# A wait between two stages of swapped halves: VectorE copies replaced by an empty TensorE instruction

## The chip, the cores and the metric

The kernel runs on one core of a Trainium2 chip. The metric is the device time of one execution in microseconds, as the median of several runs. Before the change it is 2585.78 us (three runs, 2584.07 to 2587.34). All times below are in us unless ns is written.

## The reference

The block takes x (2048 rows of 576), a fused weight for queries, keys and values, an output weight, and three weights of a gated feed-forward layer of width 4608.

```python
xn = _layernorm(x, axis=-1)
s = _A_ref(xn, A_wqkv, A_wo)               # 32 heads of 18, softmax over 2048 keys, then @ wo
g = _silu(_B_ref(xn, B_w_gate, B_w_up, B_w_down))   # (gelu(xn @ w_gate) * (xn @ w_up)) @ w_down
return x + s * g
```

Everything is float32 in and out.

## The kernel before

**Numbers.** Each float32 operand of the large products is split into a high and a low float16 part, and a product is the sum of three float16 products: high by high, high by low, low by high. For a contraction of 576 rows that makes 12 products over four full blocks of 128 rows and one or two more for the last 64 rows.

**Halves.** TensorE's rows are used as two halves of 64. A product whose operands lie on partitions 0 to 63 runs in the upper half at the same time as one on partitions 64 to 127 in the lower half. The kernel keeps the two from writing the same PSUM bank at once: two results are built together, in two banks. In stage 0 the upper half adds its 64 contraction rows to result one and the lower half adds its rows to result two; in stage 1 the halves are swapped, the upper one adding to result two and the lower one to result one. Three classes work so: `Pair` (L462; queries and keys, gate and up; tiles ma and mb, 14 slots in stage 0 and 13 in stage 1, products at L492), `DownPair` (L730; the down projection, one two-bank tile md, 6 slots of 288 columns in each stage, products at L752), and `OutPair` (L878; the output projection, either md or ma and mb, 14 slots or 17, products at L931). There are 160 such pairs, 288 down pairs and 16 output pairs in the program.

**The swap.** Stage 1's first product writes a bank that stage 0's last product, in the other half, has just written. Before stage 1 the kernel therefore waits until that last product is in. It does so with `touch` (L456 to L460): VectorE copies one element, or one from each of the two banks, out of PSUM into a small tile. The copy waits for the last product that wrote the bank, and the first product of stage 1, which writes the bank that the copy reads, waits for the copy. An output pair in two tiles, whose two halves end at different slots, copies from the bank or the banks that matter.

**Order.** The order of all instructions is written out by hand; each engine works its own queue in that order. The main loop goes over pairs of heads. At each step TensorE computes a score block for the exponentials (`qk2`, L1395, read by ScalarE's exponential at L1401), then one for the row maxima of a later pair of heads (`qk1`, L1343, read by VectorE's reduction at L1346), then part of the feed-forward work: perhaps one stage of a down pair (`DownPair.run`), then some slots of the pair in hand (`g_run`). Every five steps or so a burst (L1420) multiplies the collected exponentials with the values. A pair's stage 1 does not begin before another score block has been issued since its stage 0 ended (`blocks[0] <= gs.end`), so some other work of TensorE lies between the two stages of nearly every pair.

**The planner.** How many slots and which stages of down pairs go into each step of a stretch is chosen by `make_plan`. It tries all layouts of 4 to 7 steps and takes the one with the least sum, most of which comes from `lost`, a model of when TensorE and VectorE would be free. In it a down stage that does not end its pair, and the end of a pair's stage 0, keep VectorE until the products are done plus TOUCH:

```python
if d:
    vec = max(vec, e1 + D_STAGE) + (EVAC if late else TOUCH)
...
elif first:
    vec = max(vec, t) + TOUCH
```

**The end.** After the feed-forward layer come the output pairs, between the last score blocks and bursts of the last pair of heads; the gate (L795, L799), the evacuation of an output pair (L968, L975) and the normalisation of the last heads (L1443 to L1452) run on ScalarE and VectorE in between.

Of the kernel before, what the change touches and what calls it, by code (L numbers as in the profile page):

```python
# [12 lines left out]
F32 = mybir.dt.float32  # L13
# [81 lines left out]
def kernel(ctx: ExitStack, tc: tile.TileContext, x, wqkv, wo, w_gate, w_up, w_down, out):  # L95
    nc = tc.nc
# [4 lines left out]
    sm = ctx.enter_context(tc.tile_pool(name="sm", bufs=3))  # L101
    wp = ctx.enter_context(tc.tile_pool(name="wp", bufs=2))
    ap = ctx.enter_context(tc.tile_pool(name="ap", bufs=2))
# [349 lines left out]

    banks = deque([("ma", "mb")])

    def touch(ap):  # L456

        t = sm.tile([1, 2], F32, tag="touch", name="touch", bufs=2)
        o = t[:, 0:1] if len(ap.shape) == 2 else t.rearrange("p (a b) -> p a b", a=2)
        nc.vector.tensor_copy(o, ap)  # L460

    class Pair:  # L462

# [23 lines left out]

        def slot(self):

            for o, terms in self.q:  # L490
                lw, xx = terms[self.k]
                nc.tensor.matmul(  # L492
                    o, lw, xx, start=self.stage == 0 and self.k == 0,
                    stop=self.stage == 1 and self.k == self.slots - 1, skip_group_check=True,
                )
            self.k += 1
            if self.k < self.slots:
                return False
            if self.stage == 0:
                touch(self.b.t[0:1, 0:1])  # L500
            self.stage += 1
            if self.stage == 2:
                self.end(self.a, self.b)
            return True
# [225 lines left out]
    class DownPair:  # L730
# [8 lines left out]
        def run(self):  # L739

            w, c, sb, si = self.args
            hs = hstate[c, sb]
            sl = slice(P * si, P * si + P)
            if self.stage == 0:
                self.t = MTile("md", [P, 2, 512], F32, 1)
            k = 0
            for ft in range(2):
                for a, b in ((hs.hi, w.dhi), (hs.hi, w.dlo), (hs.lo, w.dhi)):
                    for half in range(2):
                        r = slice(64 * half, 64 * half + 64)  # L750
                        hf = half ^ self.stage
                        nc.tensor.matmul(  # L752
                            self.t.t[:, hf, 0:288], a[r, ft, sl], b[r, ft, 288 * hf:288 * hf + 288],
                            start=self.stage == 0 and k == 0, stop=self.stage == 1 and k == 5,
                            skip_group_check=True,
                        )
                    k += 1
            if self.stage == 0:
                touch(self.t.t[0:1, :, 0:1])
            self.stage += 1  # L760
            return self.stage == 2

# [115 lines left out]
    class OutPair:  # L878
# [47 lines left out]
        def slot(self):  # L926

            for half, (o, terms) in enumerate(self.q):
                if self.k < len(terms):
                    a, b = terms[self.k]  # L930
                    nc.tensor.matmul(  # L931
                        o, a, b, start=self.stage == 0 and self.k == 0,
                        stop=self.stage == 1 and self.k == len(terms) - 1, skip_group_check=True,
                    )
                    last = half
            self.k += 1
            if self.k < self.slots:
                return False
            if self.stage == 0:
                if self.wide:  # L940
                    touch(self.t[0].t[0:1, :, 0:1])
                else:
                    for o in self.o[1:] if last else self.o[::-1]:
                        touch(o[0:1, 0:1])
            self.stage += 1
            if self.stage == 2:
                self.evac()
            return True
# [283 lines left out]
    with tc.manual_schedule():  # L1232
# [23 lines left out]
        for t in range(2):  # L1256
            ln_scale(t)
            ln_hi(t)
            ln_lo(t)
        stats(7)  # L1260
        run(pw[:5])
        ln_tr(0)
        ln_out(0)
        run(pw[5:6])
        stats(4)
        run(pw[6:8])
        for t in range(2, 4):
            ln_scale(t)
# [258 lines left out]
    k = 0  # L1527
# [35 lines left out]
    dn = None  # L1563
    gs.closed = False
    G_SLOT, D_STAGE, BLOCK, BURST = 0.2158, 0.735, 0.43, 2.9
    ROW_MAX, EVAC, ADD, TOUCH = 1.28, 0.86, 0.75, 0.15
    LEAD = 0
    KEEP_HALF, KEEP_END = 2, 4
    whole = (NPAIR - 1) * 4 * NT
# [115 lines left out]
    for p in range(NPAIR):  # L1685
# [3 lines left out]
        for i in range(4 * NT):  # L1689
            s, half = divmod(i, 2)  # L1690
# [175 lines left out]
```

## Time and profile before

| | |
|---|---|
| median of three runs | 2585.78 |
| lowest, highest | 2584.07, 2587.34 |
| span of the profiled execution, first to last instruction | 2583.5 |
| mean granted TensorE clock in it | 0.997 |
| TensorE busy | 2503.6 (97%), 25816 matmuls |
| VectorE busy | 1894.5 (73%), 2595 instructions |
| of this in L460's copies | 65.4, 466 instructions |
| ScalarE, GpSimd busy | 1660.4 (64%), 1536.8 (59%) |

The profile is of one execution; the page gives its span, and the runs give whole times, whose median lies 2.3 over that span. A matmul's end in the trace is modelled, and matmuls overlap, so TensorE counts as busy through short stops; the distance from one matmul's start to the next shows them. "PE" is TensorE's matmuls, "PEld" its weight loads, "DVE" VectorE, "ACT" ScalarE, "POOL" GpSimd; a name with q is the engine's sequencer. In a timeline row stand start, duration, engine, line, operation, written tile and read tiles, shape and count, and in brackets how long the engine sat idle before it and what ended that. In the view of a tile stand durations in ns (least, median, most) with first and last start, then what the engine idled for before these instructions (us, times), then who waited for them.

### The profile page before, as it was taken

The page shows a single profiled execution, that of the slowest core. Times are in us where ns is not written, and L with a number is a line of the kernel's source. Part 1 is how long each engine was busy: PE and PEld are TensorE (multiplying, and loading weights), DVE is VectorE, ACT ScalarE, POOL GpSimd, SP SyncE. Part 2 cuts the span into 40 slices and gives each one's busy share as a digit, 9 for nine tenths or more (in the row PEclk, how much of TensorE's full clock was granted, in tenths as well). Part 3 has the DMA queues.
Part 4 walks back from the last instruction along what each step waited for, and adds up shares of the span by engine and source line. Part 5 has one row for each costly group of instructions (what it writes and reads, how often), then busy time and mean ns, then how long its engine had stood idle before and what let it go on. Part 6 is the DMA issues. An engine that isn't in the chain of part 4 may idle for free.

```text
span 2583.5 us, 60864 instructions
## 1 busy us (share of the span) xinstructions
PE 2503.6 (97%) x25816; PEld 1316.9 (51%) x25816; DVE 1894.5 (73%) x2595; ACT 1660.4 (64%) x2082; POOL 1536.8 (59%) x1545
## 2 busy tenths in 40 slices
PE   7899999999999999999999999999999999999998
PEld 6554445444544454445445545454544555455555
DVE  7677768777787778777777777776777777777644
ACT  6126666766677666766666666667666666766664
POOL 4346664576357564667576675848576676757513
PEclk9999999999999999999999999999999999999999
DMA  4430121201130112111110111201111111010124
GB/s 154 132 94 21 19 55 43 75 14 29 52 87 16 22 45 63 32 38 47 19 52 16 33 40 29 56 11 37 29 34 29 38 22 45 9 49 12 37 63 139
DMA packets 134635, 118.69 MB, mean 46 GB/s; under 512 B 59691, under 2 KB 113713, under 8 KB 134362
## 3 DMA queue, kind: packets, MB, share of 16 engines
q1 hardware_dynamic: 130089, 106.39, 15.8%
q0 software_dynamic: 1568, 5.37, 0.6%
q8 instruction: 202, 3.31, 0.5%
q10 hardware_dynamic: 2704, 3.03, 0.4%
q14 instruction: 72, 0.58, 0.1%
HBM read 84.89 MB, written 29.61 MB: 44 GB/s over the span
## 4 chain that ended last, share of the span: by engine, by line
PE 82%; DVE 7%; POOL 3%; ACT 3%; issue 2%; DMA 2%; SPq 0%; ACTq 0%; POOLq 0%; DVEq 0%
PE mb_t L492 16%; PE md_t L752 15%; PE ma_t L492 15%; PE md_t L1420 9%; PE s L1395 8%; PE s L1343 8%; PE ma_t L1420 6%; DVE PM L1346 3%; ACT P L1401 1%; PE md_t L931 1%; DVE osb L1428 1%; DMA QT<-QD 1%; POOL raw_c L356 1%; PE pv_t L511 1%; PE mb_t L931 1%
## 5 line engine op out<-in xcount | busy, mean ns | idle before, releaser
L1346 DVE TENSOR_REDUCE PM<-s 128x2 f32<-128x1024 f32 x1024 | 1251.0, 1224 | 335.5 <-PE s L1343 327.6
L1401 ACT ACTIVATE P<-s,etab 128x1024 f32<-128x1024 f32 x896 | 995.6, 1112 | 590.2 <-PE s L1395 579.4
L492 PE MATMUL ma_t<-XHT,whi_c 64*128 64x512 f16 x1440 | 542.0, 376 | 4.3 <-DVE osb L1428 2.2
L492 PE MATMUL mb_t<-XHT,whi_c 64*128 64x512 f16 x1440 | 541.7, 376 | 2.3 <-DVE touch L460 1.5
L492 PE MATMUL ma_t<-XHT,wlo_c 64*128 64x512 f16 x1296 | 487.4, 376 | 0.0
L492 PE MATMUL ma_t<-XL,whi_c 64*128 64x512 f16 x1152 | 433.2, 376 | 0.0
L492 PE MATMUL mb_t<-XHT,wlo_c 64*128 64x512 f16 x1152 | 433.2, 376 | 0.0
L492 PE MATMUL mb_t<-XL,whi_c 64*128 64x512 f16 x1152 | 433.0, 376 | 0.0
L1395 PE MATMUL s<-QT,KT 56*128 56x512 f16 x2048 | 404.4, 380 | 6.6 <-ACT P L1401 2.6
L1343 PE MATMUL s<-KT,QT 54*128 54x512 f16 x2048 | 398.3, 378 | 12.0 <-DVE PM L1346 9.7
L492 PEld LDWEIGHTS <-whi_c 64*128 64x128 f16 x5184 | 273.9, 94 | 241.0 <-issue 19.3
L752 PE MATMUL md_t<-dhi_c,hhi 64*128 64x288 f16 x2304 | 341.3, 283 | 4.8 <-DVE touch L460 2.1
L752 PE MATMUL md_t<-dhi_c,hlo 64*128 64x288 f16 x2304 | 341.0, 282 | 0.0
L752 PE MATMUL md_t<-dlo_c,hhi 64*128 64x288 f16 x2304 | 340.5, 282 | 0.0
L752 PEld LDWEIGHTS <-hhi 64*128 64x128 f16 x4608 | 246.7, 94 | 140.4 <-issue 16.8
L715 POOL TENSOR_TENSOR hlo<-gv,hhi 128x512 f16<-128x512 f32 x144 | 167.3, 1162 | 215.0 <-ACT hhi L708 210.7
L693 POOL TENSOR_SCALAR tw<-tw 128x512 f32<-128x512 f32 x144 | 90.7, 630 | 341.2 <-ACT tw L686 340.9
L1420 PE MATMUL md_t<-P,VT 128*32 128x512 f32 x2472 | 291.9, 596 | 0.5 <-ACT P L1401 0.5
L1395 PEld LDWEIGHTS <-KT 56*128 56x128 f16 x2048 | 123.5, 94 | 244.2 <-issue 156.4
L680 POOL TENSOR_TENSOR tw<-gs 128x512 f32<-128x512 f32 x144 | 151.0, 1049 | 125.2 <-ACT gs L657 125.1
L772 DVE SCALAR_TENSOR_TENSOR y<-md_t,c_c,y 128x576 f32<-128x576 f32 x272 | 219.5, 807 | 8.2 <-PE md_t L752 8.2
L492 PEld LDWEIGHTS <-wlo_c 64*128 64x128 f16 x2592 | 138.0, 94 | 118.9
(270 smaller groups left out, 4061.5 us busy)
## 6 DMA issues: line engine op xcount, KB each, us to landing
draw_c<-in_B_w_down SPq DMA_DIRECT2D x18, 576.0 KB
raw_c<-in_B_w_gate SPq DMA_DIRECT2D x18, 512.0 KB
raw_c<-in_B_w_up SPq DMA_DIRECT2D x18, 512.0 KB
obr<-rd SPq DMA_DIRECT2D x30, 256.0 KB
KT<-KD SPq DMA_DIRECT2D x32, 224.0 KB
QT<-QD SPq DMA_DIRECT2D x32, 216.0 KB
VS<-vst POOLq DMA_DIRECT2D x16, 304.0 KB, 2.6
VT<-VS SPq DMA_DIRECT2D x16, 304.0 KB
```

Source lines behind the costliest of these rows:

```text
L492: nc.tensor.matmul(o, lw, xx, start=self.stage == 0 and self.k == 0, stop=self.stage == 1 and self.k == self.slots - 1, skip_group_check=True,
L680: gp.tensor_tensor(st["t"], st["g"], st["g"], op=ALU.mult)
L693: gp.tensor_scalar(st["t"], st["t"], 1.0, 1.0, op0=ALU.mult, op1=ALU.add)
L715: gp.tensor_tensor(hs.lo[:, ft], st["v"], hs.hi[:, ft], op=ALU.subtract)
L752: nc.tensor.matmul(self.t.t[:, hf, 0:288], a[r, ft, sl], b[r, ft, 288 * hf:288 * hf + 288], start=self.stage == 0 and k == 0, stop=self.st ...
L772: nc.vector.scalar_tensor_tensor(yy, y, w.c, yy, op0=ALU.mult, op1=ALU.add)
L931: nc.tensor.matmul(o, a, b, start=self.stage == 0 and self.k == 0, stop=self.stage == 1 and self.k == len(terms) - 1, skip_group_check=True,)
L1343: nc.tensor.matmul(s1[:, h], QT[p][r, P * qt:P * qt + P], KT[p][r, 512 * kb:512 * kb + 512], start=True, stop=True)
L1346: nc.vector.tensor_reduce(PM[p][:, :, qt, kb:kb + 1], s1, op=ALU.max, axis=AX.X)
L1395: nc.tensor.matmul(s2[:, h], KT[p][r, P * kt:P * kt + P], QT[p][r, 512 * qb:512 * qb + 512], start=True, stop=True)
L1401: nc.scalar.activation(pt, s2, AF.Exp, scale=ETAB[j0])
L1420: nc.tensor.matmul(t.t[qd:qd + 32, :], VT[p][:, c0:c0 + 32], pt[:, h], start=kt == k0, stop=kt == k1, skip_group_check=True,)
```

## The change

The copies go. In their place `follow` puts an empty instruction on TensorE's own queue just ahead of stage 1's first product, and makes it wait for the last product of stage 0, which each class now remembers in `self.last`. `nofuse` keeps the instruction from being folded into a neighbour. In an output pair `last` is the last product issued in either half. The planner's TOUCH becomes zero. The rest of the program text is the same.

```diff
-    def touch(ap):
-
-        t = sm.tile([1, 2], F32, tag="touch", name="touch", bufs=2)
-        o = t[:, 0:1] if len(ap.shape) == 2 else t.rearrange("p (a b) -> p a b", a=2)
-        nc.vector.tensor_copy(o, ap)
+    def follow(earlier):
+
+        tc.add_manual_dep(
+            nc.tensor.nop(hint="swap", nofuse=True).ins, earlier.ins.name,
+            mybir.DependencyInfo(mybir.DependencyClass.Sync, mybir.DependencyReason.DATA),
+            reason="the halves change banks",
+        )
...
         def slot(self):
 
-            for o, terms in self.q:
+            for half, (o, terms) in enumerate(self.q):
                 lw, xx = terms[self.k]
-                nc.tensor.matmul(
+                if self.stage and half == self.k == 0:
+                    follow(self.last)
+                m = nc.tensor.matmul(
                     o, lw, xx, start=self.stage == 0 and self.k == 0,
                     stop=self.stage == 1 and self.k == self.slots - 1, skip_group_check=True,
                 )
...
             if self.stage == 0:
-                touch(self.b.t[0:1, 0:1])
+                self.last = m
...
-                        nc.tensor.matmul(
+                        if self.stage and half == k == 0:
+                            follow(self.last)
+                        m = nc.tensor.matmul(
                             self.t.t[:, hf, 0:288], a[r, ft, sl], b[r, ft, 288 * hf:288 * hf + 288],
...
             if self.stage == 0:
-                touch(self.t.t[0:1, :, 0:1])
+                self.last = m
...
-                    nc.tensor.matmul(
+                    if self.stage and half == self.k == 0:
+                        follow(self.last)
+                    m = nc.tensor.matmul(
                         o, a, b, start=self.stage == 0 and self.k == 0,
                         stop=self.stage == 1 and self.k == len(terms) - 1, skip_group_check=True,
                     )
-                    last = half
+                    last = m
...
             if self.stage == 0:
-                if self.wide:
-                    touch(self.t[0].t[0:1, :, 0:1])
-                else:
-                    for o in self.o[1:] if last else self.o[::-1]:
-                        touch(o[0:1, 0:1])
+                self.last = last
...
-    ROW_MAX, EVAC, ADD, TOUCH = 1.28, 0.86, 0.75, 0.15
+    ROW_MAX, EVAC, ADD, TOUCH = 1.28, 0.86, 0.75, 0.0
```

## The prediction

> **What bounds the kernel now.** I read the page first, then busy time by stage, then the view of the tile the copies write, and last the timeline around single swaps.
>
> ```profile
> span 2583.5 us, 60864 instructions
> PE 2503.6 (97%) x25816; PEld 1316.9 (51%) x25816; DVE 1894.5 (73%) x2595; ACT 1660.4 (64%) x2082; POOL 1536.8 (59%) x1545
> 250.00:600.00 350.00, 345.32 (x3510) 1.00 0.16 39
> 600.00:1000.00 400.00, 392.29 (x4011) 1.00 0.17 42
> 1000.00:1500.00 500.00, 492.06 (x5021) 1.00 0.15 40
> 1500.00:2000.00 500.00, 495.04 (x5168) 1.00 0.13 31
> 2000.00:2400.00 400.00, 396.35 (x4138) 1.00 0.11 28
> ```
>
> The five windows give, in this order, their bounds, length, TensorE's busy time (matmuls), granted clock, DMA share and GB/s. From 250 to 2400 us it is idle 4.7 + 7.7 + 7.9 + 5.0 + 3.7 = 29 us of 2150. So TensorE sets the end, and whatever VectorE does is worth only what TensorE is made to wait for it. VectorE's 73% busy is no gain in itself.
>
> The copies:
>
> ```profile
> L460 DVEq EVENT_SEMAPHORE  x337: 21/21/21, 214.1 to 2547.4; - x169
> L460 DVE COPY touch<-md_t x294: 135/138/149, 224.3 to 2569.3; 1x2 f32<-1x2 f32 x147
> L460 DVE COPY touch<-mb_t x169: 134/146/148, 151.8 to 2574.9; 1x1 f32<-1x1 f32 x169
> ...
>   PE mb_t L492: 21.0, 58
>   PE md_t L752: 19.0, 43
> ...
>   POOL E_c L326: 7.2, 3
>   PE md_t L931: 2.7, 2
>   PE mb_t L492: 2.3, 7
>   PE mb_t L931: 2.2, 3
>   PE md_t L752: 2.1, 2
>   PE pv_t L492: 0.6, 1
> ```
>
> With three more copies (two of ma_t, one of pv_t) there are 466, of about 0.14 us: 65 us of VectorE, plus 337 semaphore instructions of 21 ns (7 us) and 47 us in which VectorE stands idle at the head of its queue until TensorE's last product is in (40 us of it in the two rows quoted). The last five PE rows are what TensorE visibly pays: 9.9 us. There are 464 swaps: 160 projection and gate/up pairs, 288 down pairs, 16 output pairs (two of these copy twice).
>
> **Where a copy costs TensorE, and where not.** A swap that is covered:
>
> ```profile
> 1007.32 0.29 PE L752 MATMUL md_t<-dhi_c,hlo 64*128 64x288 f16 x2
> 1007.65 0.15 DVE L460 COPY touch<-md_t 1x2 f32<-1x2 f32 x1 [0.29 <-PE md_t L752]
> 1007.66 0.38 PE L1343 MATMUL s<-KT,QT 54*128 54x512 f16 x2
> 1007.67 0.32 PEld L752 LDWEIGHTS <-hhi 64*128 64x128 f16 x4
> 1007.88 0.29 PE L752 MATMUL md_t<-dhi_c,hhi 64*128 64x288 f16 x2
> ```
>
> The last product of stage 0 starts at 1007.32 and ends at 1007.61; two score blocks run meanwhile; the copy is through at 1007.80, and stage 1 starts at 1007.88, the usual 0.22 us after the score block. Nothing is lost. A swap that is not:
>
> ```profile
> 1495.90 0.29 PE L752 MATMUL md_t<-dhi_c,hlo 64*128 64x288 f16 x2
> ...
> 1496.24 0.38 PE L1343 MATMUL s<-KT,QT 54*128 54x512 f16 x2
> 1496.30 1.22 DVE L319 TENSOR_SCALAR E_c<-mg_c 128x2 int32<-128x2 int32 x1
> ...
> 1497.51 0.14 DVE L460 COPY touch<-md_t 1x2 f32<-1x2 f32 x1
> 1497.57 1.20 DVE L1346 TENSOR_REDUCE PM<-s 128x2 f32<-128x1024 f32 x1
> 1497.70 0.30 PE L752 MATMUL md_t<-dhi_c,hhi 64*128 64x288 f16 x2 [1.07 <-DVE touch L460]
> ...
> 1499.94 0.40 PE L1343 MATMUL s<-KT,QT 54*128 54x512 f16 x2
> ```
>
> The product was in at 1496.19, but the copy stood behind 1.22 us of other VectorE work; TensorE began 0.05 us after the copy's end, 1497.70 - 1496.24 - 0.22 = 1.24 us late. The idle column shows 1.07 of this, because the modelled end of the previous matmul covers about 0.16. So I count from start to start, less the usual spacing after that block (0.22 after a score block, 0.12 after a 288-column pair), over all swaps whose stage 1 begins within 60 ns of their copy's end. There are 50; the first and the last:
>
> ```profile
> 151.77 0.14 DVE L460 COPY touch<-mb_t 1x1 f32<-1x1 f32 x1 [0.31 <-PE mb_t L492]
> 151.97 0.37 PE L492 MATMUL mb_t<-XHT,whi_j 64*126 64x512 f16 x1
> 2574.92 0.14 DVE L460 COPY touch<-mb_t 1x1 f32<-1x1 f32 x1 [0.30 <-PE mb_t L931]
> 2575.12 0.28 PE L931 MATMUL mb_t<-whi_wo,ohl 64*128 64x288 f16 x1 [0.23 <-DVE touch L460]
> ```
>
> Their excess is 7.2 us in 25 pair swaps, 3.8 in 16 down swaps and 6.1 in 9 output swaps: **17.1 us**. That is the whole direct price of the copies.
>
> **What is added: 464 empty instructions on TensorE's queue.** Each waits until the last product of stage 0 is in, and nothing behind it is issued before: the weight loads and products of stage 1, then the next score block, for which ScalarE (exponentials) and VectorE (row maxima) wait. No DMA hangs on that queue's place. What counts is L, the time from the modelled end of the last product to the start of the first of stage 1. The trace has no such instruction; the nearest row is a semaphore wait on the same queue:
>
> ```profile
> L1420 PEldq EVENT_SEMAPHORE  x17: 51/51/51, 218.9 to 2552.7; - x17
> ```
>
> It takes 51 ns (VectorE's takes 21). Around it I put what the copies show: about 40 ns from a product's end to the copy's start (1007.61 to 1007.65), and 53 ns from its end to the matmul. So L lies between 0.12 (40 + 21 + 53, rounded up) and, with the queue's own 51 ns and as much again to fetch the first weight load behind it, 0.19 us (40 + 51 + 51 + 53). I take **0.19**, since nothing behind the wait is prefetched. What hides it is the work between the stages. For all but 15 swaps that cover is at least 0.235 us after the last product's end (in the covered case 1007.88 - 1007.61 = 0.27; some 110 swaps lie so; some 340 have 0.4 us or more, most of them 0.9, with other products between; the 15 have one score block or none). At L = 0.12 the 15 short swaps pay 1.5 us together, at 0.19 2.6 us. If the cover is outrun it costs: at 0.30, 7 us over 119 swaps; at 0.38, 17; at 0.50, 33.
>
> [...]
>
> **What is handed back.** Where TensorE no longer waits, the next thing it needs of VectorE is the row maximum of the score block it ran, behind which the copy stood. In the stall above that reduction ends at 1498.77 and the next score block starts at 1499.94, so 1.1 us earlier is possible. Over the 41 pair and down stalls the slack is at least the excess in all but a few: I take off 1.0 us.
>
> **The output stage** has the longest stop:
>
> ```profile
> 2504.43 0.40 PE L1395 MATMUL s<-QT,KT 56*128 56x512 f16 x2
> 2507.33 0.30 PE L931 MATMUL md_t<-whi_wo,ohl 64*128 64x288 f16 x2 [2.50 <-DVE touch L460]
> 2507.57 0.42 PE L931 MATMUL md_t<-whi_wo,ohl 64*128 64x288 f16 x4
> 2509.12 0.72 PE L931 MATMUL md_t<-whi_wo,ohl 64*128 64x288 f16 x4
> 2508.00:2511.30 3.30, 3.30 (x29) 2.44 (x27) 0.36 (x1) 2.08 (x3) 0.00 (x0) 0.50 0.02 5
> ```
>
> The stop is 2507.33 - 2504.43 - 0.22 = 2.68 us, and then the granted clock is 0.50 for 3.3 us (0.42 us becomes 0.72), which loses half of that, 1.7 us. Without the stop both go. But the chain of gate, evacuation and next burst behind it still runs on ScalarE and VectorE; I take off 1.3 us for that in this stage.
>
> [...]
>
> **The planner's constant.** TOUCH goes from 0.15 to 0 in the sums by which each stretch of 4 to 7 steps is laid out. The order of some stretches will change, by differences of at most 0.15 per down start or gate/up swap in a sum that stays otherwise the same. What it can move is the idle time that remains: from 250 to 2400 us 29 us, of which the copies' stalls in those windows are about 8.5. I value it at nothing and keep 7 us (a third of the rest) either way for the range.
>
> **The freed VectorE time** (119 us) meets TensorE's other waits for VectorE only where a copy stands just ahead of the late result; I take 0, with 4 us at most.
>
> **The sum**: 17.1 + 1.7 (clock) - 2.6 (rest of the wait) - 1.0 - 1.3 = 13.9 us less. The span becomes 2583.5 - 13.9 = 2569.6. The timed runs before have a median of 2585.78, 2.3 us over the span of the profiled execution (start and end around it), which stays: 2571.9, **2572 us**, 0.5% faster.
>
> **Rivals.**
> 1. *The stall is handed on.* VectorE is late with the same work, so TensorE next waits for the row maximum instead. Then each of the 41 stalls gains only the copy's 0.14 us: 5.7, less 2.6 for the wait, 3.1: 2583. For it: the reductions follow the copies without a gap (1497.57). Against: the slack of 1.1 us at 1499.94.
> 2. *The wait is dearer than its cover*, which is the slower side: the queue behind the empty instruction restarts slowly, and about 120 swaps with only the score blocks between their stages pay L - 0.27 each. The gross gain without the term for the rest of the wait is 16.5; it is used up at L = 0.38. At 0.50 the swaps pay 33: 2585.8 + 16.2 = 2602. Against it stand the 51 ns row and, at 218.9, that semaphore waits on this queue run ahead of the products. Were the queue emptied at each swap, score blocks included, every swap would stop for some 0.38 us and the time would be about 2750; I give that 2 of 100 within this case.
> 3. *The new order is worse.* The re-planned stretches add as much idle time as the steady part has beside the copies, 29 - 8.5 = 20 us: 2572 + 20 = 2592; half of it: 2582.
> 4. *The gain is larger*: the order and the freed VectorE each give their bound, 2572 - 7 - 4 = 2561.
> 5. *No wait is put on the instruction* (the dependency lies within one engine). Then the rest of the wait goes too, 2569, inside the forecast.
>
> **Chances.** Forecast, 2565 to 2579: 55. Rival 4: 10. Rival 1: 17 (12 within 0.2%, 5 below). Rival 2: 8. Rival 3: 10 (5 within, 5 slower). A measurement of this kernel tells about 0.2%, 5.2 us, from no change. So faster 0.55 + 0.10 + 0.05 = 0.70; same 0.12 + 0.05 = 0.17; slower 0.08 + 0.05 = 0.13. For 8 in 10 the range goes from rival 4's bound, 2560, to past rival 1 and half of rival 3: 2588.
>
> **What would show it.** No copies at L460; VectorE busy near 1829 us; 464 more entries on TensorE's queue, some 50 ns each. At the late swaps the first product of stage 1 follows the score block by 0.22 us. No half clock near 2508. PE's idle time from 250 to 2400 falls from 29 to about 21 us. I am wrong if the first products of covered swaps come 0.3 us or more after the score block (L too small), if waits for L1346 rise by as much as the copies' go (handed on), or if idle time rises at other places (order).

## The result, and the profile after

The changed kernel takes 2568.68 us (median of five runs, 2568.55 to 2572.9) against 2585.78: the ratio is 0.9941, with a 95% interval of 0.993 to 0.9951. That is about 17 us, or 0.6%. The forecast was 2572 us, 14 us less than before. Of all executions of the kernels below one, of order_alone, was far slower than its fellows (2779.96 us, at a mean granted clock of 0.893, the others at 0.997), and it is left out of its ratio.

The page of the changed kernel, its first two lines of numbers:

```profile
span 2566.9 us, 60550 instructions
PE 2495.3 (97%) x25816; PEld 1301.0 (51%) x25816; DVE 1854.4 (72%) x2129; ACT 1662.3 (65%) x2082; POOL 1540.4 (60%) x1545
```

The 466 copies are gone from VectorE (2595 instructions became 2129). Its busy time fell by only 40 us, although the copies measured 65: a copy overlapped the instruction behind it (in the prediction's rows, 1497.51 + 0.14 = 1497.65, and the reduction begins at 1497.57), and the page counts such a stretch once.

Busy time by stage, in the five steady windows (bounds, length, TensorE's busy time and matmuls, the same for weight loads, VectorE, ScalarE and GpSimd, then granted clock, DMA share and GB/s):

```profile
250.00:600.00 350.00, 344.56 (x3508) 171.79 (x3502) 259.62 (x291) 233.00 (x270) 209.53 (x211) 1.00 0.17 39
600.00:1000.00 400.00, 393.41 (x4027) 200.07 (x4025) 299.23 (x338) 276.34 (x378) 234.42 (x243) 1.00 0.17 43
1000.00:1500.00 500.00, 493.46 (x5065) 243.42 (x5063) 375.57 (x412) 334.81 (x389) 323.52 (x319) 1.00 0.15 39
1500.00:2000.00 500.00, 494.96 (x5156) 248.08 (x5154) 368.35 (x397) 343.00 (x452) 339.13 (x333) 1.00 0.14 31
2000.00:2400.00 400.00, 397.11 (x4132) 206.32 (x4128) 292.33 (x313) 268.07 (x312) 265.54 (x260) 1.00 0.11 29
```

TensorE is idle 5.4 + 6.6 + 6.5 + 5.0 + 2.9 = 26.5 us in them; before it was 29. The fall is small because much of a stall was never counted as idle, as the prediction said of the modelled ends. Some of the rest isn't the kernel's doing. Three stops depend on when transfers between the engines' memories and DRAM land, and they differ from run to run (over the traces of thirteen kernels the wait at the first of the three is 0.38 to 2.46 us). One of them in the changed kernel, from its timeline:

```profile
330.08 0.29 DVE L309 TENSOR_REDUCE mg_j<-mb_j 128x1 f32<-128x128 f32 x1 [2.46 <-DMA mb_j<-mxd_j]
...
331.80 0.39 PE L1347 MATMUL s<-KT,QT 54*128 54x512 f16 x2 [1.77 <-DVE PM L1350]
```

VectorE waited 2.46 us for a transfer, the row maxima behind it came late, and TensorE lost 1.77 us. At the same place of the program the kernel before lost less: the same reduction waited 0.80 us, the copy stood behind it, and TensorE stood idle for 0.55 us. Elsewhere it lost 1.34 us, again behind such a transfer:

```profile
333.16 0.29 DVE L309 TENSOR_REDUCE mg_j<-mb_j 128x1 f32<-128x128 f32 x1 [0.80 <-DMA mb_j<-mxd_j]
...
333.80 0.37 PE L492 MATMUL mb_t<-XHT,whi_c 64*128 64x512 f16 x1 [0.55 <-DVE touch L460]
...
615.16 0.28 DVE L309 TENSOR_REDUCE mg_j<-mb_j 128x1 f32<-128x128 f32 x1 [3.75 <-DMA mb_j<-mxd_j]
...
616.35 0.37 PE L492 MATMUL ma_t<-XHT,whi_c 64*128 64x512 f16 x1 [1.34 <-DVE osb L1428]
```

Where VectorE's freed time went stands in the view of groups; the last two columns are its idle time ahead of the row maxima, and what ended it. First before, then after:

```profile
L1346 DVE TENSOR_REDUCE PM<-s 128x2 f32<-128x1024 f32 x1024 | 1251.0, 1224 | 335.5 <-PE s L1343 327.6
```

```profile
L1350 DVE TENSOR_REDUCE PM<-s 128x2 f32<-128x1024 f32 x1024 | 1251.1, 1224 | 397.2 <-PE s L1347 389.2
```

The reductions take the same 1251 us. VectorE now waits 61.6 us longer for TensorE's score blocks. Freed time on the engine that is not the bottleneck turned into waiting for the bottleneck.

### The profile page after: what moved, and what is told of

It is laid out like the page before. It is cut to its first block, busy times and chain, and to the rows that moved or that the text cites. A ratio compares the mean times of both kernels' runs of the same rounds, so it can differ in the third digit from the quotient of the medians.

```text
span 2566.9 us, 60550 instructions
## 1 busy us (share of the span) xinstructions
PE 2495.3 (97%) x25816; PEld 1301.0 (51%) x25816; DVE 1854.4 (72%) x2129; ACT 1662.3 (65%) x2082; POOL 1540.4 (60%) x1545
## 4 chain that ended last, share of the span: by engine, by line
PE 84%; DVE 6%; POOL 3%; ACT 3%; DMA 2%; issue 2%; SPq 0%; ACTq 0%; POOLq 0%; DVEq 0%
PE mb_t L496 16%; PE ma_t L496 16%; PE md_t L758 15%; PE md_t L1424 10%; PE s L1399 8%; PE s L1347 8%; PE ma_t L1424 7%; DVE PM L1350 2%; ACT P L1405 1%; DMA QT<-QD 1%; DVE osb L1432 1%; POOL raw_c L356 1%; PE pv_t L515 1%; PE md_t L939 1%; PE mb_t L1424 1%
## 5 line engine op out<-in xcount | busy, mean ns | idle before, releaser
L1347 PE MATMUL s<-KT,QT 54*128 54x512 f16 x2048 | 399.0, 377 | 13.0 <-DVE PM L1350 10.6
```

What stands on the lines that cost most here:

```text
L1347: nc.tensor.matmul(s1[:, h], QT[p][r, P * qt:P * qt + P], KT[p][r, 512 * kb:512 * kb + 512], start=True, stop=True)
```

## The experiments

Twelve kernels ran, on three chips; each is compared with the kernel before on its own chip (medians 2582.43, 2583.94 and 2582.97 us).

**1 and 2. The planner's constant against the instruction.** The first kernel is the changed one with the old constant, so its instruction order is that of before. The second has the copies, and only the constant changed.

```diff
 # order_kept, against the changed kernel
-    ROW_MAX, EVAC, ADD, TOUCH = 1.28, 0.86, 0.75, 0.0
+    ROW_MAX, EVAC, ADD, TOUCH = 1.28, 0.86, 0.75, 0.15
 # order_alone, against the kernel before
-    ROW_MAX, EVAC, ADD, TOUCH = 1.28, 0.86, 0.75, 0.15
+    ROW_MAX, EVAC, ADD, TOUCH = 1.28, 0.86, 0.75, 0.0
```

> The empty instructions, but TOUCH stays 0.15, so that the planner lays out the steps as in the kernel before. Theory (the gain is TensorE's wait for late copies): nearly the whole gain stays, about 2570 us (17.1 us of stalls less some 1.2 for the rest of the wait). Rival (the new order of the steps brought a good part of it): 2575 us or more.

> The copies as before, only TOUCH is 0. Theory: the order alone brings nothing, 2586 us, within 3 us. Rival (the order brought it): 2575 to 2580 us.

Measured: order_kept 2567.69 us, ratio 0.9941 (0.9927 to 0.9954), the gain of the whole change. Order_alone 2586.07 us, ratio 1.001 (1.0001 to 1.0019). The new order brings nothing; alone it costs about 0.1% if anything. The whole gain is the instruction's.

Because order_kept has the matmuls of the kernel before in the same order, each can be set against itself. The late swap that the prediction quoted (its first product at 1497.70) now reads so, in the timeline of order_kept:

```profile
1487.08 0.29 PE L758 MATMUL md_t<-dhi_c,hlo 64*128 64x288 f16 x2
...
1487.42 0.38 PE L1347 MATMUL s<-KT,QT 54*128 54x512 f16 x2
1487.48 1.22 DVE L319 TENSOR_SCALAR E_c<-mg_c 128x2 int32<-128x2 int32 x1
...
1487.64 0.29 PE L758 MATMUL md_t<-dhi_c,hhi 64*128 64x288 f16 x2
...
1488.68 1.21 DVE L1350 TENSOR_REDUCE PM<-s 128x2 f32<-128x1024 f32 x1
```

VectorE's 1.22 us are still there. The first product of stage 1 no longer stands behind them: it follows the score block by 0.22 us (before: 1.46). The long stop of the output stage went the same way:

```profile
2491.15 0.40 PE L1399 MATMUL s<-QT,KT 56*128 56x512 f16 x2
2491.44 0.30 PE L939 MATMUL md_t<-whi_wo,ohl 64*128 64x288 f16 x2
...
2492.05 0.42 PE L939 MATMUL md_t<-whi_wo,ohl 64*128 64x288 f16 x4
```

From 2.90 us between the starts to 0.29; the four products of the last row take 0.42 us, where 0.72 stood at half clock. The window of 3.3 us from there on has the full clock (0.50 before):

```profile
2492.10:2495.40 3.30, 3.30 (x55) 2.79 (x50) 2.86 (x5) 3.30 (x6) 0.00 (x0) 1.00 0.02 5
```

The half clock does not follow every such stop, though. In order_alone and pairs_only, which keep the stop, the granted clock is 0.50 behind it, as before; in downs_only of experiment 5, which keeps it too, the clock stays at 1.00:

```profile
2499.69 0.40 PE L1405 MATMUL s<-QT,KT 56*128 56x512 f16 x2
2502.58 0.30 PE L941 MATMUL md_t<-whi_wo,ohl 64*128 64x288 f16 x2 [2.50 <-DVE touch L468]
2502.80:2506.10 3.30, 3.30 (x55) 2.86 (x52) 0.87 (x2) 2.17 (x4) 0.00 (x0) 1.00 0.02 5
```

Each of these traces is of one execution, and what decides between the two is open.

Set against each other by stage, with the direct stalls that the prediction counted in the trace of before (worked out from the starts of the same matmuls in both traces):

```
us of before    direct stalls   order_kept is ahead by   of it, transfers that landed otherwise
0 - 250              2.3              2.4
250 - 600            2.1              1.8                 -0.4 (near 331)
600 - 1000           0.8              2.9                 +1.5 (at 616), +0.9 (at 905)
1000 - 1500          3.0              2.5
1500 - 2000          0.7              0.4
2000 - 2400          1.9              1.3
2400 - end           6.3              6.1
sum                 17.1             17.3                 +2.0
```

Near 331 order_kept gained 0.71 us where the copy had been late, and lost 0.64 at the next score block, whose row maxima stood behind the same reduction. Against the products the transfer landed 0.37 us later than before; the other 0.27 us are the stall handed on to the row maxima.

So the kernel itself is 17.3 - 2.0 = 15.3 us faster in this pair of executions, and it is faster where the copies were late.

**3. Is the wait on TensorE real, and what is L?** Each empty instruction waits for the newest product on the queue, the score blocks included, so that nothing covers it.

```diff
-            nc.tensor.nop(hint="swap", nofuse=True).ins, earlier.ins.name,
+            nc.tensor.nop(hint="swap", nofuse=True).ins, newest[0].ins.name,
```

> The empty instruction waits for the newest product issued before it, mostly the score block between the stages, in place of stage 0's last product: the cover is gone. With 0.11 us from a product's end to the first product behind the instruction (trace of the kernel after), each swap should stop for 0.38 + 0.11 - 0.22 = 0.27 us, 464 times 125 us: about 2690 us. Rival (the queue needs longer to restart, 0.2 to 0.3 us): 2735 to 2780 us; if the wait were not real: 2569 us.

Measured: 2691.03 us, ratio 1.042 (1.0401 to 1.0439). In the spans that is 2687.9 - 2566.9 = 121 us, or 0.26 us for each of the 464 swaps. The wait is put on the instruction and holds TensorE's queue. What keeps it free in the changed kernel is the work between the stages.

L itself is read where no work lies between the stages. The view of line 459, and one such swap, both of the changed kernel:

```profile
L459 PEldq NOP  x464: 13/13/13, 149.7 to 2558.6; - x155
```

```profile
2542.60 0.28 PE L939 MATMUL md_t<-wodh,onl 64*128 64x288 f16 x1
2542.99 0.30 PE L939 MATMUL md_t<-whi_wo,ohl 64*128 64x288 f16 x2
```

The product's modelled end is 2542.60 + 0.28 = 2542.88, the next start 2542.99: L = 0.11 us. In the trace the empty instruction starts some 42 ns after the end, and 69 ns after its own start the first product begins. Late first products come to about 1.2 us in all: twice 0.27 us in the output stage, and 11 times 0.05 to 0.08.

**4. What an empty instruction costs beside its wait.** Three more, or one more, behind each, waiting for nothing.

```diff
+        for _ in range(3):        # one_more: range(1)
+            nc.tensor.nop(hint="pad", nofuse=True)
```

> As the kernel after, with three more empty instructions, without a wait, behind each one that waits. Theory (cheap against the cover of 0.27 us): at 13 to 51 ns each they add 0.04 to 0.15 us to the 0.11, so only the swaps without full cover pay: 0.5 to 3 us more than after, 2569 to 2572 us. Rival (cover nearly used up, each one dear): 10 us or more, 2579 us and above.

> The changed kernel with one further empty instruction behind each of the 464, which waits for nothing. In the run with three further ones each took some 71 ns on TensorE's queue, so the time from the last product to the first of stage 1 was about 0.11 + 3 x 0.071 = 0.32 us; here it is about 0.18, close to the 0.19 of the prediction. Theory A (an empty instruction costs only where it outruns the work between the stages): under 2 us over the changed kernel, since only the some 15 short swaps pay 0.07 us more each, 1.1 us; ratio 0.994 to 0.995. Rival B (each empty instruction costs alike, hidden or not): a third of what three cost, 10.4 / 3 = 3.5 us; ratio 0.9955 to 0.9965.

Measured: three_more 2579.91 us, ratio 0.9988 (0.9979 to 0.9997). One_more 2570.26 us, ratio 0.9951 (0.9939 to 0.9964), beside the changed kernel's 0.9941. The same swap in both, first with one more, then with three:

```profile
2544.47 0.28 PE L941 MATMUL md_t<-wodh,onl 64*128 64x288 f16 x1
2544.94 0.30 PE L941 MATMUL md_t<-whi_wo,ohl 64*128 64x288 f16 x2 [0.19 <-PE md_t L941]
```

```profile
2552.59 0.28 PE L941 MATMUL md_t<-wodh,onl 64*128 64x288 f16 x1
2553.21 0.30 PE L941 MATMUL md_t<-whi_wo,ohl 64*128 64x288 f16 x2 [0.33 <-PE md_t L941]
```

L is 0.11 with none, 0.19 with one and 0.33 with three more: some 0.07 us each, though each shows as 13 ns. The time does not follow in proportion. One more is 1.9 us over the changed kernel in the spans (2568.8 against 2566.9), of which 1.2 had arisen by 95 us, ahead of the first swap at 150; three more are 10.8 us over (2577.7), of which 1.1 by 95 us: 9.7 us, the rival's side of that expectation. With three, L has passed the 0.27 us that the smallest common cover gives, and the prediction's curve (7 us at 0.30, 17 at 0.38) says about 10 for 0.33. The ratio of one_more can't tell its theory A from its rival B, since the interval holds both; the trace can. Set against the changed kernel product by product, one_more loses ground for good at 14 swaps, some 0.08 us at each, 1.1 us in all, and these are swaps with too little work between their stages; with three more, over 150 swaps start late. In these runs a further empty instruction cost where L outran the cover: at 14 swaps, 1.1 us, with L = 0.19; at over 150, 9.7 us, with 0.33.

**5. The classes one by one.** Only the pairs, only the down pairs or only the output pairs get the instruction; the others keep their copies. The order is the new one in all three, so they stand beside order_alone.

```diff
 # pairs_only: in DownPair; here and in OutPair follow is gone
 # too, and OutPair has its own copies of before back
-                self.last = m
+                touch(self.t.t[0:1, :, 0:1])
```

> Same order of steps as the kernel after (TOUCH 0); only the 160 projection and gate/up pairs have the empty instruction, down and output pairs keep their copies. Theory: the pairs' stalls go, 7 us less than with all copies in this order; about 2579 us if that one is at 2586. Rival (the gain is mostly at the end of the kernel): 2 us or less.

> Only the 288 down pairs have the empty instruction. Theory: 3 to 4 us less than with all copies, about 2582 us. Rival (the copies of down pairs delay the others behind them on VectorE, so that the 288 matter more than their own stalls): 6 us or more less.

> Only the 16 output pairs have the empty instruction. Theory: 6.1 us of stalls and 1.7 us of half clock, less 1.3 for what is handed back and 1 for the rest of the wait: 5 to 6 us less than with all copies, about 2580 us. Rival (the late chain of gate and evacuation takes the stalls' place): 2 us or less.

Measured: 2579.01, 2580.4 and 2580.53 us; ratios 0.9979 (0.997 to 0.9988), 0.9989 (0.998 to 0.9998) and 0.9984 (0.9975 to 0.9992). Against order_alone's 1.001 that is about 0.31%, 0.21% and 0.26%, or 8, 5 and 7 us; their sum, 0.78%, stands beside 0.69% for the whole (1.001 - 0.9941). Each ratio has an interval of some 2.3 us on either side, and a difference of two of them some 3.3. Within that they agree with the direct stalls of 7.2, 3.8 and 6.1 us, and no class loses; the order of the classes is not shown, and the 5 us of downs_only lie between its theory (3 to 4) and its rival (6 or more) and decide nothing.

**6. Is VectorE's freed time worth anything?** The prediction valued it at nothing. The first test put 464 copies back that nothing waits for. They copy 80 constants between two tiles outside PSUM, and wait for the last product as the old ones did.

```diff
+        t = sm.tile([1, 80], F16, tag="touch", name="touch", bufs=2)
+        c = nc.vector.tensor_copy(t, cst[0:1, 0:80])
+        tc.add_manual_dep(
+            c.ins, earlier.ins.name,
+            mybir.DependencyInfo(mybir.DependencyClass.Sync, mybir.DependencyReason.DATA),
+            reason="waits as the old copy did",
+        )
```

> The empty instructions, and besides them on VectorE one small copy per swap at the old place, which waits for the same last product as the old copy but reads a constant, so that nothing waits for it. VectorE has its load and its idle time at the head of its queue back. Theory (only what TensorE waits for counts): 2569 to 2571 us. Rival (freed VectorE time is part of the gain): some 5 us or more come back, 2574 us or above.

Measured: 2579.95 us, ratio 0.9991 (0.9982 to 1.0). In the spans 9.8 us of the gain came back: the rival's side, and the prediction's zero seemed to have fallen. The view of the tile shows that the test wasn't what it was meant to be (least, median and longest duration in ns):

```profile
L459 DVE COPY touch<-cst x464: 160/172/1706, 149.0 to 2568.7; 1x80 f16<-1x80 f16 x155
```

The old copies took 134 to 149 ns. Of these, 164 took over 200, up to 1706. One of them in the timeline:

```profile
1492.65 1.26 POOL L698 TENSOR_TENSOR gv<-gv,gs 128x512 f32<-128x512 f32 x1
1492.70 1.25 DVE L459 COPY touch<-cst 1x80 f16<-1x80 f16 x1
...
1493.87 1.21 DVE L1363 TENSOR_REDUCE PM<-s 128x2 f32<-128x1024 f32 x1
...
1495.13 0.39 PE L1360 MATMUL s<-KT,QT 54*128 54x512 f16 x2 [1.06 <-DVE PM L1363]
```

GpSimd's instruction ends at 1493.91, the copy at 1493.95. The row maxima behind it end 1495.08, and TensorE, which in the changed kernel does not stop here, waits 1.06 us. Of the 164 long copies 160 ended 32 to 40 ns after an instruction of GpSimd, and in 158 of these GpSimd had started first. Why a copy lasts until then no run here shows. Three further kernels took apart what it costs: the same copies with no wait at all, and reductions of two constants in their place, with the wait and without it.

```diff
 # copies_free: the copy without add_manual_dep
 # maxima_unwaited: the reduction with it; maxima_free: without it
-        c = nc.vector.tensor_copy(t, cst[0:1, 0:80])
+        c = nc.vector.tensor_reduce(t[:, 0:1], unit, op=ALU.max, axis=AX.X)
```

> The changed kernel with the 464 unwaited copies of 80 constants, now waiting for nothing at all. If the lengthening beside GpSimd is what cost 10 us: the copies are still up to 1 us or more long in the trace, and the ratio is 0.997 to 1.000 (5 to 12 us over the changed kernel). If it was the wait for the last product: copies of 0.16 us, ratio 0.994 to 0.995.

> The changed kernel with 464 small VectorE reductions (a maximum over two constants, one partition) where the old copies stood; each waits for the last product of stage 0 as the old copy did, and nothing waits for it. In the run with unwaited copies 10 us came back, but there the copies took 160 to 1706 ns instead of 134 to 149, and the long ones ended some 36 ns after an instruction of GpSimd: the copy out of the constant was not the old copy. Theory A (that lengthening was the price; VectorE's freed time in itself is worth nothing, as predicted): no more than 2 us over the changed kernel, ratio to the kernel before 0.994 to 0.995, reductions of 0.15 us, waits of TensorE for the row maxima near 11 us. Rival B (0.15 us and the wait at the head of VectorE's queue do cost): 5 to 10 us over the changed kernel, ratio 0.996 to 0.998, waits for the row maxima 13 us or more and new waits ahead of down products.

> The same 464 reductions, waiting for nothing: VectorE's 65 us of busy time come back without the wait at the head of its queue. Theory A (freed time is worth nothing): ratio 0.994 to 0.995, as in the run with the wait. If the run with the wait is dearer by more than 3 us, the price is the wait at the head of the queue; if both stand 5 us or more over the changed kernel, it is the busy time.

Measured: copies_free 2579.98 us, ratio 0.9988 (0.9979 to 0.9997); maxima_unwaited 2569.97 us, 0.9951 (0.9939 to 0.9964); maxima_free 2567.63 us, 0.9944 (0.9932 to 0.9957). The view of the tile in copies_free and in maxima_unwaited:

```profile
L459 DVE COPY touch<-cst x464: 161/166/1679, 149.7 to 2567.1; 1x80 f16<-1x80 f16 x155
```

```profile
L462 DVE TENSOR_REDUCE touch<-unit x464: 131/132/145, 153.0 to 2561.4; 1x1 f32<-1x2 f32 x155
  PE mb_t L509: 21.7, 59
  PE md_t L772: 18.7, 43
```

The reductions are what the old copies were, in length and in waiting at the head of the queue (21.7 and 18.7 us ahead of them, where the prediction's rows of the old copies have 21.0 and 19.0), and they cost no more than the intervals can tell: 0.001 against the changed kernel's ratio, and in the trace nothing between 250 us and the end, where maxima_unwaited goes from 3.6 us behind the changed kernel to 2.7. Of the 3.6, 3.3 had arisen by 95 us, ahead of the first swap; there the granted clock was 0.50 for 10.2 us, against 6.8 in the changed kernel. The copies without any wait are as dear as those with it. So the price was the lengthening beside GpSimd, not VectorE's busy time and not its wait. The places say so too: set against the changed kernel product by product, copies_unwaited falls back in 27 steps of more than 0.15 us; ahead of 26 of them, by less than 4 us, stands a copy of over 0.4 us, and these 26 make some 11 us (the 4 us behind such copies cover a fifth of the time). TensorE's waits for the row maxima show a part of it, in the kernel before, the changed kernel, copies_unwaited and maxima_unwaited, in this order (us, times, longest):

```profile
PE s L1343 <- DVE PM L1346: 9.7, 16, 1.5
```

```profile
PE s L1347 <- DVE PM L1350: 10.6, 17, 1.8
```

```profile
PE s L1360 <- DVE PM L1363: 13.5, 26, 1.5
```

```profile
PE s L1363 <- DVE PM L1366: 9.7, 15, 1.8
```

## Why the prediction was right, and by how much it was off

**The bound.** TensorE sets the end. The 61.6 us by which VectorE now waits longer for score blocks, and the reductions of experiment 6, show that this much of VectorE's time has no price that the runs can tell.

**Direct stalls, 17.1 us.** Right in place, and in sum within what was handed back: the table by stage has 17.1 beside 17.3, or 15.3 without the transfers. The single swaps quoted moved from 1.46 to 0.22 us and from 2.90 to 0.29.

**The rest of the wait, 2.6 us at L = 0.19.** This term was mis-sized. L is 0.11, just below the lower bound of 0.12 (114 ns before rounding up), and the rest of the wait about 1.2 us. The bound added a matmul's 53 ns to an instruction's 21, and the value taken added a queue's 51 ns twice, the second time for fetching the first weight load; that was an estimate, and no run times that step by itself. The trace has 42 + 69: at the swap quoted in experiment 3 the weight load starts 38 ns after the empty instruction, and the product 31 ns after the load. That nothing behind the wait is prefetched, the reason given for the larger value, the trace of the changed kernel shows for the weights: at all 448 pair and down swaps the first load of stage 1 starts 80 ns or more after the end of the last product; in the kernel before it starts ahead of that end at 14 of them. The cover was sized rightly: at L = 0.33 three_more lost 9.7 us behind the first swap, where the curve had about 10.

**The clock, 1.7 us.** Right in this pair: no half clock in the window that answers to 2508. But I took it for certain that the half clock belongs to the stop, and downs_only has the stop without it. That the term came out whole is in part luck.

**Handed back, 2.3 us.** The direct stalls, the clock and the rest of the wait make 17.1 + 1.7 - 1.2 = 17.6; without the transfers the pair of executions shows 15.3. What is left over, 2.3 us, is what the 1.0 + 1.3 taken for this foresaw; it is a remainder, and only the 0.27 us near 331 were read off at their place. TensorE's waits for the row maxima went from 9.7 to 8.5 us in order_kept and to 10.6 in the changed kernel, where 1.8 is the late transfer at 331: rival 1, that most of the stalls are handed on, did not come.

**The planner's order, nothing.** Right: order_kept and the changed kernel have the same ratio.

**The sum.** 13.9 forecast; 1.4 more from the smaller L and 2.0 from transfers that landed otherwise make 17.3, which is what the spans of before and of order_kept differ by (2583.5 - 2566.0 = 17.5, first and last instructions included). So 1.4 us of the error is mine, and the rest lies within what executions of one kernel differ by: the timed runs of the changed kernel span 4.4 us.

**What was named as a sign and was wrong.** VectorE's busy time fell to 1854 us, not 1829: the copies were taken off at their full length, though their overlap with the instruction behind them goes on being counted. The 464 entries show 13 ns, not 50, though each holds the queue for some 70. TensorE's idle time fell to 26.5 us, not 21: the stalls were taken off at their full length though only a part of each shows as idle, and the transfer at 331 added to it.

Of the other rivals, the dearer wait (2) needs an L of 0.38 to break even (its 16.2 us at L = 0.50 should read 33 - 16.5 = 16.5; the 2602 stands). Three_more, at 0.33, had a ratio of 0.9988 and so nearly reached that point. Rival 3 falls with order_kept, rival 4 because neither of its two terms, the order and the freed time, brought anything, and rival 5 with wait_for_newest.

## What to carry to other kernels

The copies, which only order two instructions of TensorE, were paid for at the 50 of 464 swaps where they came late (17.1 us), as behind 1.22 us of other work on VectorE's queue; count such places, start to start, and leave the engine's busy time out of the sum (464 small reductions put back moved the ratio by 0.001 at most from that of the changed kernel). The wait on TensorE's own queue showed no cost where the work already issued outlasted it (0.11 us, against a cover of 0.235 or more at all but 15 swaps), and 0.26 us a swap where it was for the newest product; so size that cover for every place and see how many places share the smallest. When an experiment puts an instruction back, look at its duration in the trace before believing its time (160 to 1706 ns here, where 134 to 149 were meant).

## What the runs showed of the hardware

An empty instruction on TensorE's queue is recorded as 13 ns, but adds about 70 ns to the distance between the products around it (0.11, 0.19 and 0.33 us with none, one and three more).

VectorE's small copy between tiles outside PSUM grew from 0.16 to as much as 1.7 us beside GpSimd; the old copy out of PSUM (134 to 149 ns) and the small reduction (131 to 145 ns) did not, in the same places: 196 of the 466 old copies lay wholly inside an instruction of GpSimd, and of the 464 new ones 16. The long instruction behind which the quoted copy of before stood fits this; it is usually short (168 ns least, 170 median):

```profile
1496.23 1.26 POOL L682 TENSOR_TENSOR tw<-tw,gs 128x512 f32<-128x512 f32 x1
```

```profile
L319 DVE TENSOR_SCALAR E_c<-mg_c x18: 168/170/1221, 125.8 to 2218.8; 128x2 int32<-128x2 int32 x18
```

GpSimd's instruction ran from 1496.23 to 1497.49, and the 1.22 us of L319 from 1496.30 to 1497.52. Two of the 18 are this long, and both end 24 ns after an instruction of GpSimd. By these times the wait of 1.24 us at this swap came from GpSimd, through VectorE's queue to a copy, and through the copy to TensorE; no run changed GpSimd's instruction to test it. The change did not take that wait away (it is still 1.22 us in order_kept), only TensorE's place behind it.
